# A chunked recurrence followed by a gated MLP: three whole PSUM regions, one step each, and a new order of the pieces

## Chip, cores and metric

One core of a Trainium2 chip runs the kernel; the metric is device microseconds of one execution. Engines are named as in the profile: PE (matmuls), PEld (its weight loads), DVE (VectorE), ACT (ScalarE), POOL (GpSimd), SP (the queue that issues the DMAs).

## The reference

Four batches, eight heads, 768 steps, head size 40. For each batch and head a 40x40 state is carried over the steps; then the outputs of all heads form one row of 320 numbers per step, which goes through a gated MLP.

```
for t in range(768):                       # state: (4, 8, 40, 40)
    y[t]  = r[t] @ state
    Sa    = state @ a[t]
    state = state * w[t] - outer(Sa, b[t]) + outer(v[t], k[t])
h = gelu(x @ w_in); u, v = h[:, :512], h[:, 512:]     # x: 320, h: 1024
out = x + (u * (w_sg @ layernorm(v) * g_ln + b_sg)) @ w_out
```

## The kernel before

The 768 steps are cut into 12 units of 64 (`c` = 0 to 11), and each unit is worked on for four batches (`b` = 0 to 3), eight heads at once. `attention` (L160) builds three kinds of work for a unit.

**Gates**, four per unit, one for each batch (L324 to L407). `gate_w` squares the decays on ACT; `gate_1` scans them on DVE into `ex`; `gate_r` copies the totals to `call` (ACT, into the PSUM tile `fixed[1]`) and takes their reciprocals (DVE); `gate_2` makes `ae`; `gate_3` scans backwards into `hs`, which lies in the same tile `fixed[1]`, makes `kb` (DVE) and issues the load of a later `main`; `gate_4` is 32 matmuls into `pa`, called AB here; `gate_a`, `gate_n` and `gate_k` read AB out of `pa` into `ks` (DVE), `nts` and `kbt` (ACT).

**The inverse**, one per unit for all four batches. `lift` (two ACT copies) and `inv_in` (DVE transposes `nts` into `n`) start a triangular solve of 31 steps. Steps 0 to 28 are a product and an add each on POOL (58 instructions, scratch tile `tg`); the last `LAST` = 2 steps are three small DVE instructions, `by_col` (L446), called column steps here: one scalar_tensor_tensor on 15 or 16 elements for each column that is left. `inv_back` transposes the result twice (`x1z`, `xt`); `inv_g` and `inv_x` are 64 small matmuls each into `pa` (G and X), and `inv_h` and `inv_y` copy them out on ACT (`gs`, `xt`).

**The chain**, fourteen pieces for each unit and batch (`chain`, L645), which carry the state: K and R (`k_mm`, `r_mm`) into `pb`, read by ACT as `past` and `rb`; U into `pb`, read by ACT as `u`; S into `pa`, read by four ACT instructions as `sc`, the state; UT into `pc`, read by ACT as `ut`; P into `pc`, read by DVE as `pqs`; Y into `pc`, read by DVE as `yt`, which SP stores to `xd`. Each of `pa`, `pb`, `pc` is one tile of two PSUM banks, so `pa` serves AB, G, X and S of all batches, `pb` K, R and U, `pc` UT, P and Y.

The order of all this is a list. Each piece has a position (`CHAIN[b]`, `GATE[b]`, `BACK`, `JOIN`, `SOLVE`, `LIFT`, plus 28 per unit); the pieces are sorted by it and tried in turn (L907 to L917). A piece raises `Later` when something it needs has not been issued (`need`) or its place is taken (`take`); it is held and tried again first after every piece that went out. A very early position therefore means "as soon as its needs are met". The instructions of each engine run in the order in which this list emits them. `ahead` (L170) stretches positions below `AHEAD[0]`.

The MLP's preparation (weights split into high and low halves, `Mlp.side`, L1268) is placed in the same list by `DEC`, `PX`, `PV`, `FILL` and others, in the last three units; the MLP itself (`Mlp.run`, L1329) follows in the fixed orders `SEQ0`, `SEQ` and `SEQL`.

```
take("ab", 3)                                   # gate_4: AB's place in pa
take("SP")                                      # s_mm: S's place, also in pa
n = NP * (C + 1)
ones, rc, hsp = fixed[0][:, 0:n], fixed[0][:, n - C:2 * n - C], fixed[1][:, 0:n]
call = fixed[1][:, n:n + NCH * B * NP].rearrange("p (i q) -> p i q", q=NP)
```

Of the kernel before, what the change touches and what calls it, by code (L numbers as in the profile page):

```python
# [32 lines left out]
WARM = 14  # L33
NTS, NX = 4, 3
RING, RING1, FREED = 19, 16, (36, 40)
PZERO = (-30.57, -38.88)
LX = -31.5
LV = -27.58
LR = -24.52
ZERO = (-32.44, -14.72)  # L40
BLANK = (-31.08, -10.75)
IDS = -22.74
HEAT = ((13.9, 11),)
GATE0 = ((0.31, 0, -11.54, -2.54, -8.03, 1.82, 1.17, 2.22, 1.26), (0.03, 0, 0.3, 0.68, -5.12, 1.72, 2.12, 3.36, 2.83))
EW = (1.0, 1.24)
EB = (-31.98, -28.48)
EE = (('GGGG', 'GVGG'), ('GGGG', 'GGGV'))
SUB0 = (-24.73, -24.68, -15.2, -21.18, -15.71)
BACK0 = (-14.34, 0.27)
SOLVE1 = (-14.12, 0.5)  # L50
C10 = -16.81
GATE = ((-91.34, -95.51, -87.94, -87.58, -89.37, -86.29, -82.36, -84.74, -85.37), (-85.42, -83.72, -82.19, -80.33,
    -75.21, -78.25, -71.62, -74.78, -90.65), (-82.7, -77.04, -75.4, -74.24, -72.07, -69.43, -67.72, -63.9, -67.03),
    (-72.51, -74.0, -78.05, -71.52, -74.69, -62.51, -61.13, -75.25, -58.26))
GE = "VVVV"
AHEAD = (19.95, 0.67)
# [10 lines left out]
LIFT = (-59.11, -59.44)  # L67
CG = 0.7978845608028654
G1 = 0.044715
GEND, AEND, IEND = 246.0, (266.0, 294.0), 312.5  # L70
PIN = 266.02
DSTEP = ((-13.06, -3.36, 0.0, 0.13, 3.41, 3.62), (-16.79, -1.11, 0.0, 0.61, 3.02, 3.47))
DEC = ((275.89, 0), (276.24, 0), (284.23, 0), (286.85, 0), (290.7, 1), (297.59, 1), (298.13, 1), (306.35, 0),
    (309.82, 0), (317.07, 1), (323.45, 0), (329.7, 1))
PX = 270.05
PV = 294.03
PL = 335.9
FILL = (("x0", 0, 319.86), ("v0", 0, 331.35), ("v1", 0, 344.98), ("v2", 0, 346.14), ("u0", 0, 349.9))
AFTER = {"v": (0.56, 0.57, 1.47, 1.57, 2.13, 2.48, 2.96, 4.17, 5.19), "u": (1.14, 1.97, 2.82, 3.17), "x": ()}
EARLY = 4  # L80
PSG = 313.1
SGD = (-6.74, -0.32, 1.37)
# [18 lines left out]
JUNK = ((294.28, 5), (295.93, 4), (307.25, 6), (312.36, 3), (312.43, 1), (346.91, 3), (349.9, 4))  # L101
# [58 lines left out]
def attention(tc, a, xd, flag, keep, ps, mlp):  # L160
# [16 lines left out]
    with ExitStack() as ctx:  # L177
# [12 lines left out]
        (pa, pb, pc), slots_end = ps.slots(ctx)  # L190
        fixed, fixed_end = ps.fixed(ctx)

        def gt_end():
            need(*every(("ks", NCH - 1), ("n", NCH - 1), ("kt", NCH - 1)))
            A.copy(out=calls, in_=call.rearrange("p i q -> p (i q)"))
# [13 lines left out]
        mains = static("main", 4, [128, ML], gt)  # L209
# [29 lines left out]
        def main_of(i):  # L239
            return mains[i % 4]  # L240
# [22 lines left out]
        def drop(x):  # L263
            live[x] -= 1

        def warmup(n):
            take("PQ", 0)
            for _ in range(n):
                T.matmul(pc[:, 0, 0:128], lhsT=warm, rhs=warm, start=True, stop=True, skip_group_check=True)
# [30 lines left out]

        spread([lambda: V.memset(pa[:, :, 4 * R104:], 0.0), lambda: V.memset(pb[:, :, 0:4 * D], 0.0), lambda: V.memset(pc, 0.0)] + [lambda t=t: V.memset(t, 0.0) for t in rbs], *PZERO)
        spread([lambda k=k: clear16(xts[k][:, :, 0:32]) for k in range(2)] + [lambda f=f, h=h: clear(f, h) for f in range(2) for h in range(2)], *ZERO)
        spread([lambda: G.memset(gz, 0.0)] + [lambda t=t: G.memset(t, 0.0) for t in scs], *BLANK)

        for i, t in enumerate(aes):
            at(EB[i // 4] + EW[i // 4] * (i % 4 + 0.6) if i < 8 else IDS + i, lambda t=t: A.copy(out=t[:, :, C:C + D], in_=bc(id40.unsqueeze(1), [128, NP, D])))

# [14 lines left out]
        kbs, unit, x1_of, pqt = {}, {}, {}, {}  # L322

        def gate_w(c, b):  # L324
            i = c * B + b
            before(c, b, 4, "kb")
            wv = main_of(i)[:, 1:WL].rearrange("p (q x) -> p q x", x=C + 1)[:, :, 0:C]
            A.activation(out=junk, in_=wv, func=AF.Square, accum_out=wsum[:, i:i + 1])
            seen.add(("w", c, b))

        def gate_1(c, b):
            before(c, b, 4, "kb")
# [5 lines left out]
        def gate_r(c, b):  # L338
            i = c * B + b
            need(("g1", c, b))  # L340
# [13 lines left out]
        def gate_3(c, b, E=V):  # L354
            i = c * B + b
            need(("gr", c, b), ("w", c, b), ("ae", c, b))
            before(c, b, 2, "ab")
            drop("rc")
            w = main_of(i)[:, 0:WL]
# [4 lines left out]
            kb = kbs[c, b] = gt.tile([128, 2, NP, C], F32, name="kb", bufs=2)  # L364
            hv = hs[:, :, 1:C + 1].unsqueeze(1).broadcast_to([128, 2, NP, C])
            E.tensor_tensor(out=kb, in0=kab[:, 0:3:2], in1=hv, op=ALU.mult)
            load_main(i + 4)
# [15 lines left out]
        def pav(x):  # L383
            return pa[:, :, 2 * R104 * x:2 * R104 * x + 2 * R104].rearrange("p h (j w) -> p h j w", j=2)[:, :, :, 0:C]

        def gate_a(c, b):
            need(("ab", c, b))
            before(c, b, RING1, "k")
            V.tensor_tensor(out=kss[ent1(c, b)], in0=pav(0), in1=bc(mask.unsqueeze(1).unsqueeze(1), [128, 2, 2, C]), op=ALU.mult)
            seen.add(("ks", c, b))  # L390
            drop("ab")

        def gate_n(c, b):
            need(("ab", c, b))
            if c >= NTS:
                need(("gp", c - NTS))
            A.mul(out=nts[c % NTS][:, 4 * b:4 * b + 4].rearrange("p (h j) t -> p h j t", h=2), in_=pav(1), mul=-1.0)
            seen.add(("n", c, b))
            drop("ab")

        def gate_k(c, b):
            need(("ab", c, b))
            before(c, b, RING, "yp")
            A.copy(out=kbts[ent(c, b)][:, 0:DM].rearrange("p (h i d) -> p h i d", h=2, i=4),
                   in_=pa[:, :, 0:4 * R104].rearrange("p h (i w) -> p h i w", w=R104)[:, :, :, C:R104])
            seen.add(("kt", c, b))
            drop("ab")  # L407
# [108 lines left out]
        def join16(c):  # L516

            nt, xt = nts[c % NTS], xts[c % 2]
            p = [x.rearrange("p (q t) -> p q t", q=NQ) for x in (pa[:, 0, 0:256], pa[:, 1, 0:256], pa[:, 0, 256:512])]


            def first():
                need(("x1", c))
                take("ab")
# [7 lines left out]
            def lower():  # L532
                need(("j1", c))
                drop("ab")
# [3 lines left out]
            def second():  # L538
                need(("j2", c))
                take("ab", 2)  # L540
# [12 lines left out]
            def add_t():  # L553
                need(("j3", c))
                drop("ab")
# [5 lines left out]
            def add_x():  # L561
                need(("j3", c))
                drop("ab")
# [6 lines left out]
        def inv_back(c, k):  # L570
# [11 lines left out]
            else:  # L582
                need(("x1", c) if c else ("ax", c))
# [17 lines left out]
        def inv_h(c):  # L601
            need(("gp", c), *((("xp", c - 1),) if c else ()))
            drop("ab")
# [5 lines left out]
        def inv_x(c):  # L609
            need(("gs", c), ("xc", c, 0), ("xc", c, 1))  # L610
            take("ab")
# [8 lines left out]
        def inv_y(c):  # L620
            need(("xp", c))
            drop("ab")
# [857 lines left out]
```

## Time and profile before

| | |
|---|---|
| runs (us) | 791.82, 793.41, 802.39; median 793.41 |
| profiled execution (us) | 805.59; its span 803.9 |
| PE busy | 599.9 us (75%), 14292 matmuls |
| DVE busy | 482.4 us (60%), 950 instructions |
| ACT busy | 339.7 us (42%), 1001 instructions |
| POOL busy | 354.3 us (44%), 842 instructions |
| mean granted clock of PE | 0.802 |

Busy time is the time in which an engine has at least one instruction under way. A wait is an engine's idle time in front of an instruction, put down to what released it. The chain that ended last follows the run back from its last instruction, at each step to what released it or to the instruction before it on its engine. The granted clock is the share of PE's full speed; its two levels are 1.2 and 2.4 GHz. The windows view cuts the span into stretches.

### The profile page before, as it was taken

Reading aid. Unit: us, or ns where it says so; the run is one execution under the profiler, and the core shown is the slowest. Engines: PE = TensorE matmul, PEld = TensorE weight load, DVE = VectorE, ACT = ScalarE, POOL = GpSimd, SP = SyncE. Lnnn points to the kernel's source line nnn. Section 1 sums busy time; section 2 is a strip of 40 time slices with the busy share of each in tenths; the row PEclk is TensorE's granted clock in tenths of the full one; section 3 lists DMA queues with packets and bytes.
Section 4 is the critical chain, followed back from the end, with each engine's and each line's share of the span. In section 5 each row is a group of like instructions: output and inputs, shape, how many; then the busy total and the mean of one; then the engine's idle time right before and its main releaser. Section 6 shows DMA issues by size and latency. Waiting matters only on the chain.

```text
span 803.9 us, 32652 instructions
## 1 busy us (share of the span) xinstructions
PE 599.9 (75%) x14292; PEld 555.5 (69%) x14292; DVE 482.4 (60%) x950; ACT 339.7 (42%) x1001; POOL 354.3 (44%) x842
## 2 busy tenths in 40 slices
PE   4445657576758475867576777768799999999997
PEld 4345557575747464767476766656699899999996
DVE  5554774647473837373835244555898876866843
ACT  3543435444444444444443343433644453443520
POOL 4625694636372736372728402022535433323331
PEclk7555667876887888868886666857989999999999
DMA  4411223232323222323112322312420020110001
GB/s 167 126 42 52 73 64 93 65 90 65 90 65 92 63 90 65 93 62 92 47 45 65 93 79 71 106 32 77 145 74 7 25 84 26 36 49 25 25 1 55
DMA packets 38872, 54.58 MB, mean 68 GB/s; under 512 B 19712, under 2 KB 30464, under 8 KB 38720
## 3 DMA queue, kind: packets, MB, share of 16 engines
q1 hardware_dynamic: 38720, 52.40, 22.1%
q8 instruction: 114, 1.87, 1.0%
q14 instruction: 38, 0.31, 0.1%
HBM read 44.52 MB, written 7.86 MB: 65 GB/s over the span
## 4 chain that ended last, share of the span: by engine, by line
PE 57%; DVE 21%; ACT 12%; issue 6%; DMA 1%; POOL 1%; SPq 0%; DVEq 0%; ACTq 0%; POOLq 0%
PE pa L146 15%; PE sg L146 13%; PE pc L146 8%; PE pb L146 7%; PE op L146 5%; PE hv L146 5%; DVE x L146 5%; PE hu L146 4%; DVE pqs L146 2%; DVE ks L146 2%; DVE fixed L146 2%; ACT sc L146 2%; DVE n L146 2%; ACT gs L146 2%; ACT nts L146 1%
## 5 line engine op out<-in xcount | busy, mean ns | idle before, releaser
L146 POOL TENSOR_TENSOR tg<-x,n 128x126 f32<-128x126 f32 (+24 forms) x334 | 118.8, 366 | 177.9 <-DVE n L146 165.2
L146 POOL TENSOR_TENSOR x<-x,tg 128x126 f32<-128x126 f32 (+24 forms) x334 | 120.0, 370 | 12.0
L146 PE MATMUL pa<-ae,kb 64*64 64x104 f32 x1536 | 63.1, 319 | 38.2 <-ACT nts L146 8.0
L146 PEld LDWEIGHTS pa<-ae,kb 64*64 64x64 f32 x1536 | 51.4, 178 | 43.9 <-POOL ae L146 11.7
L146 DVE TENSOR_TENSOR_SCAN fixed<-main,fixed 128x260 f32<-128x260 f32 x42 | 29.1, 693 | 70.7 <-ACT fixed L146 70.4
L146 PE MATMUL sg<-wsh,vh 128*128 128x384 f32 x192 | 66.0, 344 | 4.5 <-ACT wsh L146 4.5
L146 DVE TENSOR_TENSOR pqs<-pc,mask 128x512 f32<-128x512 f32 x48 | 32.9, 685 | 58.9 <-ACT ut L146 34.6
L146 PE MATMUL sg<-wsl,vh 128*128 128x384 f32 x192 | 65.7, 342 | 0.4 <-POOL wsl L146 0.4
L146 PE MATMUL sg<-wsh,vl 128*128 128x384 f32 x192 | 65.6, 342 | 0.0
L146 POOL TENSOR_TENSOR gx<-g,gy 128x384 fp32r<-128x384 f32 x30 | 31.7, 1060 | 64.5 <-ACT gy L146 64.5
L146 PE MATMUL pb<-vs,ks 64*64 64x40 f32 x768 | 43.1, 268 | 13.9 <-ACT u L146 8.8
L146 PEld LDWEIGHTS pb<-vs,ks 64*64 64x64 f32 x768 | 38.9, 181 | 17.0 <-ACT u L146 11.5
L146 ACT ACTIVATE sc<-pa,ex 104x40 f32<-104x40 f32 x176 | 37.2, 296 | 26.0 <-PE pa L146 25.3
L146 PE MATMUL pa<-x1z,nts 32*32 32x32 f32 (+1 forms) x896 | 23.1, 225 | 33.2 <-DVE x1z L146 31.8
L146 ACT COPY rb<-pb 128x320 f32<-128x320 f32 (+1 forms) x48 | 20.1, 418 | 65.1 <-PE pb L146 65.1
L146 POOL TENSOR_TENSOR lt<-lt,sc 128x256 f32<-128x256 f32 (+1 forms) x11 | 6.7, 612 | 90.2 <-ACT lt L146 42.2
L146 PEld LDWEIGHTS pa<-x1z,nts 32*32 32x32 f32 x896 | 21.4, 143 | 34.8 <-DVE x1z L146 33.1
L146 PE MATMUL pc<-rv 64*64 64x64 f32 x768 | 26.0, 257 | 25.4 <-ACT ut L146 24.4
L146 PE MATMUL pc<-rv,rb 64*64 64x64 f32 x704 | 24.8, 270 | 26.2 <-DVE pqs L146 26.2
L146 DVE TENSOR_TENSOR yt<-pc,ex 104x256 f32<-104x256 f32 x48 | 19.5, 407 | 41.1 <-PE pc L146 25.0
L146 PE MATMUL pb<-rb,xt 64*64 64x40 f32 x768 | 40.8, 255 | 3.6 <-ACT rb L146 2.6
L146 DVE SCALAR_TENSOR_TENSOR x<-x,n 128x15 f32<-128x15 f32 (+2 forms) x34 | 42.1, 1242 | 0.4
(169 smaller groups left out, 1772.2 us busy)
## 6 DMA issues: line engine op xcount, KB each, us to landing
main<-main SPq DMA_DIRECT2D x88, 160.8 KB
rv<-rv SPq DMA_DIRECT2D x48, 240.0 KB
vs<-vb SPq DMA_DIRECT2D x24, 160.0 KB
xd<-yt SPq DMA_DIRECT2D x96, 40.0 KB
xt<-xd SPq DMA_DIRECT2D x16, 192.0 KB
out<-y SPq DMA_DIRECT2D x16, 192.0 KB
ws<-wst SPq DMA_DIRECT2D x12, 192.0 KB
main<-first SPq DMA_DIRECT2D x4, 514.5 KB
```

Of the source, the lines that this page charges most:

```text
L146: return self.tc.keep_in_program_order(f(*a, **k))
```

## The change

PSUM: the three two-bank tiles are now three equal regions (`slots` 0, 1, 2), and a table `SLOT` gives every step of every batch one of them whole. `hold` takes the region before the matmuls, `free` gives it up with the last reader. No two steps share a region at a time in the list. `call` moves from `fixed[1]` in PSUM to `calls` in SBUF, so ACT no longer writes the tile that DVE's `hs` scans write; the copy of `call` at the end of the gates is gone.

Buffers: `main` has six tiles in place of four (`NM`; the six are loaded whole at the start), `kb` four in place of two (`NK`), the POOL scratch three in place of two.

Solve: `LAST` = 3, so steps 0 to 27 are on POOL (56 instructions), and six column steps on DVE end it.

Order: all positions of the recurrence are new, most of them far below zero. Clearing the regions and scratch tiles is now something that the first users `need`. `k_mm` waits in the list for S and Y of its own batch in the unit before, in place of U of the batch before; U opens its own accumulation. The 11 warm-up matmuls of `HEAT` are gone. The positions of the MLP's preparation move by a few units at most; the MLP's own order is the same.

```diff
+SLOT = {'AB': [0, 2, 1, 0], 'G': [0], 'X': [1], 'R': [1, 2, 1, 2], 'U': [0, 2, 1, 1], 'SP': [0, 1, 0, 1], 'UT': [2, 1,
+    0, 2], 'PQ': [1, 0, 2, 0], 'YP': [2, 2, 2, 2]}
 NTS, NX = 4, 3
+NM, NK = 6, 4
-HEAT = ((13.9, 11),)
+HEAT = ()
-GATE = ((-91.34, -95.51, -87.94, -87.58, -89.37, -86.29, -82.36, -84.74, -85.37), (-85.42, ...
+GATE = ((-110.27, -128.96, -296.34, -114.57, -150.08, -85.83, -81.69, -262.03, -432.92), (-68.4, ...
-CHAIN = ((-1.17, -5.94, 1.87, -10.45, -4.45, 0.8, 7.4, -4.35, -12.01, 5.4, 15.73, 10.49, 19.51, 3.41), (-6.44, ...
+CHAIN = ((-0.75, -48.5, -87.55, -1.43, -286.58, -131.61, -26.49, -93.14, -58.32, -158.08, 17.2, -33.17, 22.28,
+    -13.06), (-3.03, ...
-SOLVE = (-63.22, -55.95, 0.7)
-LAST = 2
-BACK = (1.65, 3.79, -2.9, 2.67)
-JOIN = (-5.29, -10.98, -6.3, 8.02)
+SOLVE = (-58.31, -50.2, 0.69)
+LAST = 3
+BACK = (-18.88, 3.85, 8.97, -51.07)
+JOIN = (-59.81, -24.91, -46.27, 12.87)
-        mains = static("main", 4, [128, ML], gt)
+        mains = static("main", NM, [128, ML], gt)
-        call = fixed[1][:, n:n + NCH * B * NP].rearrange("p (i q) -> p i q", q=NP)
         calls = keep.tile([128, NCH * B * NP], F32, name="calls")
+        call = calls.rearrange("p (i q) -> p i q", q=NP)
+        def hold(ph, b=0, n=1):
+            need(("pz", SLOT[ph][b]))
+            take(("s", SLOT[ph][b]), n)
+
+        def free(ph, b=0):
+            drop(("s", SLOT[ph][b]))
         def gate_4(c, b):
-            need(("kb", c, b))
-            take("ab", 3)
+            need(("kb", c, b), ("id", ent1(c, b)))
+            ...
+            hold("AB", b, 3)
+            pa = slot("AB", b)
-            R, U, SP = pb[:, :, 0:4 * D], pb[:, :, 4 * D:6 * D], pa[:, :, 4 * R104:4 * R104 + 2 * D]
-            PQ, UT, YP = pc[:, :, 0:4 * C], pc[:, :, 4 * C:6 * C], pc[:, :, 6 * C:8 * C]
+            R, U, SP = slot("R", b)[:, :, 0:4 * D], slot("U", b)[:, :, 0:2 * D], slot("SP", b)[:, :, 0:2 * D]
+            PQ, UT, YP = slot("PQ", b)[:, :, 0:4 * C], slot("UT", b)[:, :, 0:2 * C], slot("YP", b)[:, :, 0:2 * C]
             def k_mm():
                 if c:
-                    need(*([("um", c, b - 1)] if b else every(("um", c - 1))))
-                take("R")
+                    need(("sm", c - 1, b), ("yp", c - 1, b))
+                hold("R", b)
-            fs = chained(c, steps(c, 0, 31 - LAST, G, f"tg{c % 2}"), "in", "so" if LAST else "sv")
+            fs = chained(c, steps(c, 0, 31 - LAST, G, f"tg{c % NX}"), "in", "so" if LAST else "sv")
```

## Rows read from the trace of the kernel before

**Rows 1.** Windows view: busy us of each engine, granted clock, DMA share, in five stretches.

```profile
0.00:66.42 66.42, 31.67 (x764) 28.25 (x764) 36.02 (x90) 29.45 (x82) 34.01 (x112) 0.56 0.32 102
66.42:121.98 55.56, 32.70 (x934) 29.44 (x934) 37.22 (x64) 24.14 (x84) 39.38 (x113) 0.62 0.24 69
...
236.91:276.86 39.95, 26.50 (x1088) 24.45 (x1088) 23.43 (x40) 17.62 (x61) 19.56 (x58) 0.80 0.28 78
...
436.64:534.08 97.44, 71.78 (x2404) 64.94 (x2404) 41.29 (x109) 40.11 (x128) 22.92 (x47) 0.68 0.28 82
...
583.56:803.90 220.34, 213.28 (x1157) 204.42 (x1157) 158.16 (x328) 83.98 (x181) 76.20 (x86) 0.98 0.12 37
```

**Rows 2.** Chain that ended last, in order: start us, us, engine and tile.

```profile
66.42 1.94 PE pa L146 x64
...
121.98 1.94 PE pa L146 x64
...
270.87 3.48 DVE x L146
...
436.64 1.92 PE pa L146 x64
...
534.08 3.65 PE hv L146 x8
```

**Rows 3.** Waits view, 118.8 to 434 us: total us, times, longest.

```profile
DVE fixed L146 <- ACT fixed L146: 57.5, 8, 7.6
...
PE pa L146 <- DVE x1z L146: 25.8, 8, 4.2
...
PE pc L146 <- DVE pqs L146: 16.4, 16, 1.3
```

**Rows 4.** Windows view of tile pa, of pb and of pc, one unit.

```profile
236.91:276.86 39.95, 12.58 (x448) 10.68 (x448) 1.67 (x4) 8.71 (x28) 0.80 0.28 78
...
236.91:276.86 39.95, 9.28 (x256) 8.47 (x256) 0.00 (x0) 3.47 (x12) 0.80 0.28 78
...
236.91:276.86 39.95, 9.24 (x384) 7.94 (x384) 4.29 (x8) 1.56 (x4) 0.80 0.28 78
```

**Rows 5.** Column steps on VectorE: two lines by form, one of the timeline.

```profile
L146 DVE SCALAR_TENSOR_TENSOR x<-x,n 128x15 f32<-128x15 f32 x22 | 32.3, 1473 | 0.0
...
L146 DVE SCALAR_TENSOR_TENSOR x<-x,n 128x16 f32<-128x16 f32 x11 | 9.6, 872 | 0.4
...
506.71 0.52 DVE L146 SCALAR_TENSOR_TENSOR x<-x,n 128x15 f32<-128x15 f32 x2
```

**Rows 6.** Lines by form in one unit, 236.9 to 276.86 us.

```profile
L146 PE MATMUL pa<-ae,kb 64*64 64x104 f32 x128 | 4.9, 287 | 0.6 <-ACT kbt L146 0.4 <-DVE ks L146 0.2
...
L146 DVE TENSOR_TENSOR_SCAN fixed<-main,fixed 128x260 f32<-128x260 f32 x4 | 2.8, 690 | 7.3 <-ACT fixed L146 7.2
...
L146 DVE TENSOR_TENSOR kb<-main,fixed 128x512 f32<-128x512 f32 x4 | 2.7, 686 | 0.1
...
L146 DVE TENSOR_TENSOR pqs<-pc,mask 128x512 f32<-128x512 f32 x4 | 2.7, 685 | 4.4 <-ACT ut L146 3.0 <-PE pc L146 1.4
...
L146 DVE STREAM_TRANSPOSE n<-nts 128x1024 f32<-128x1024 f32 x1 | 2.0, 1972 | 0.0
...
L146 DVE TENSOR_TENSOR ks<-pa,mask 128x256 f32<-128x256 f32 x4 | 1.7, 418 | 2.1 <-ACT nts L146 2.1
...
L146 ACT ACTIVATE nts<-pa 128x256 f32<-128x256 f32 x4 | 1.6, 392 | 0.0
...
L146 ACT COPY nts<-nts 32x512 f32<-32x512 f32 x2 | 1.2, 616 | 0.0
...
L146 DVE STREAM_TRANSPOSE x1z<-x 128x512 f32<-128x512 f32 x1 | 1.0, 1041 | 0.0
```

**Rows 7.** Timeline of POOL: start us, us, instructions merged as xcount, [idle before].

```profile
266.35 0.24 POOL L146 TENSOR_TENSOR tg<-x,n 128x31 f32<-128x31 f32 x1 [18.66 <-DVE n L146]
...
270.60 0.64 POOL L146 TENSOR_TENSOR tg<-x,n 128x91 f32<-128x91 f32 x2
```

More of the change, by code (lines that the diff above doesn't have):

```diff
@@ L189, in attention @@
         gt, gt_right = pool("at_gate", "right")
-        (pa, pb, pc), slots_end = ps.slots(ctx)
+        slots, slots_end = ps.slots(ctx)
         fixed, fixed_end = ps.fixed(ctx)
         def gt_end():
-            need(*every(("ks", NCH - 1), ("n", NCH - 1), ("kt", NCH - 1)))
-            A.copy(out=calls, in_=call.rearrange("p i q -> p (i q)"))
+            need(*every(*[(x, NCH - 1 - k) for x in ("ks", "n", "kt") for k in range(4)]))
             gt_right()
@@ L264, in drop, with slot @@
             live[x] -= 1
+        def slot(ph, b=0):
+            return slots[SLOT[ph][b]]
+        def hold(ph, b=0, n=1):
[3 more added lines that the diff above has]
+            drop(("s", SLOT[ph][b]))
         def warmup(n):
-            take("PQ", 0)
+            take(("s", 2), 0)
             for _ in range(n):
-                T.matmul(pc[:, 0, 0:128], lhsT=warm, rhs=warm, start=True, stop=True, skip_group_check=True)
+                T.matmul(slots[2][:, 0, 0:128], lhsT=warm, rhs=warm, start=True, stop=True, skip_group_check=True)
         warmup(WARM)
@@ L356, in gate_3 @@
             need(("gr", c, b), ("w", c, b), ("ae", c, b))
-            before(c, b, 2, "ab")
+            need(*[("ab", *x) for x in kbo[-NK:len(kbo) - NK + 1]])
             drop("rc")
+            kbo.append((c, b))
             w = main_of(i)[:, 0:WL]
@@ L610, in inv_x @@
             need(("gs", c), ("xc", c, 0), ("xc", c, 1))
-            take("ab")
+            hold("X")
+            gv = square("X")
             xt = xts[c % 2]
@@ L711, in u_mm @@
                 need(("rb", c, b), ("xt", c))
-                take("U")
+                hold("U", b)
                 for j in range(2):
                     for y, h in ORD:
-                        mm(U[rows(y), h, D * j:D * j + D], xt[rows(y), 4 * b + 2 * h + j], right(y, h, j), y, y, not c and not j)
+                        mm(U[rows(y), h, D * j:D * j + D], xt[rows(y), 4 * b + 2 * h + j], right(y, h, j), y, y, not j)
                 seen.add(("um", c, b))
@@ L725, in ut_mm @@
                 need(("rb", c, b), ("xt", c))
-                take("UT")
+                if c:
+                    need(("pm", c - 1, b))
+                hold("UT", b)
                 for j in range(2):
@@ L788, in y_mm @@
                     raise Later
-                take("YP")
+                hold("YP", b)
                 pqs = pqt.pop(b)
@@ L1444, in lay @@
         main[:, :, WL + 256 * j:WL + 256 * (j + 1)] = em(f[k]).reshape(n, 2 * D, 256)
[L1445 removed]
+    first = np.zeros((NM, 2, 64, ML), np.float32)
     first[..., 0:WL] = 1.0
[L1447 removed]
+    first[:, :, 0:D] = main[0:NM].reshape(NM, 2, D, ML)
     def heads(x):
@@ L1456, in lay @@
     w = raw(f["moe_w_in"])
-    out = dict(main=main, first=first.reshape(4, 128, ML), rv=rows, vb=vb,
+    out = dict(main=main, first=first.reshape(NM, 128, ML), rv=rows, vb=vb,
                x0=np.eye(32, dtype=np.float32).reshape(1, 16, 2, 1, 32).transpose(0, 2, 3, 1, 4).repeat(NQ, 2).repeat(4, 0).reshape(128, NQ, 32),
```

181 lines of the change are left out of this document (93 added, 88 removed), and 3 rows, old and new, of the table CHAIN.

## The prediction

> **What bounds the kernel now.** I read the windows view first. From 583.56 us on, PE is busy 213.28 of 220.34 us at a clock of 0.98: the MLP is bound by PE, and the change doesn't touch it. Before that nothing is full. In the unit from 236.91 to 276.86 us PE is busy 26.5 of 39.95 us, DVE 23.4, POOL 19.6, ACT 17.6 [rows 1]. Then the chain that ended last: X of unit 0 starts at 66.42 us, X of unit 1 at 121.98, X of unit 9 at 436.64, and the first MLP matmul (hv) that follows the last unit at 534.08 [rows 2]. So eight units take 314.7 us, 39.3 each; the start takes 66.4, unit 0 takes 55.6, and the tail 97.4.
>
> What a unit of 39.3 us waits for stands in the waits view. Over eight units PE stood 25.8 us ahead of G for DVE's `x1z` (3.2 a unit) and 16.4 for `pqs`; DVE stood 57.5 us, 7.2 a unit, in front of `hs` scans for an ACT instruction that writes `fixed`, the tile of the scan [rows 3]. That ACT instruction is the copy to `call`. AB's matmuls wait for `kbt` and `ks`, the readers of the AB before, because all use `pa` [rows 6]. POOL stood 18.66 us in one piece for `n`, which comes at the end of the gates [rows 7]. So the unit is set by engines that pass work on in an unlucky order, through three tiles of which one carries most.
>
> How much one carries: PE, DVE and ACT work on `pa` for 12.6 + 1.7 + 8.7 = 23.0 us a unit, on `pb` for 12.8, on `pc` for 15.1 [rows 4].
>
> **The regions.** The table deals the 30 steps of a unit out as 9, 10 and 11. Priced by the old tiles (23.0/10 for a step of `pa`, 12.8/8 for `pb`, 15.1/12 for `pc`), region 0 gets 5 x 2.3 + 1.6 + 3 x 1.26 = 16.9, region 1 18.1, region 2 15.9 us [rows 4]. The fullest region falls from 23.0 to 18.1. Neither is a bound at 39 us; what the deal buys is that the next step on PE mostly goes to another region while ACT reads the last. By the positions, the run after X is U0 (region 0), UT1 (1), U1 (2), S0 (0), U2 (1), UT0 (2), UT2 (0), S1 (1), S2 (0), the digit behind a step being its batch: two steps on other regions lie between nearly all neighbours in one.
>
> **The scans' bank.** With `call` in SBUF the 7.2 us a unit of [rows 3] have no cause left: the new `hs` scan needs only DVE's own results. This is no gain by itself, since DVE is not full; it brings `kb` and so AB, `nts` and `n` earlier.
>
> **The column steps.** One more solve step goes from POOL to DVE: two POOL instructions less, three DVE instructions more. POOL is not full, so the first is worth nothing. A column step took 32.3 + 9.6 us for 33, mean 1.27; the same instruction after POOL had ended took 0.26 (0.52 for two) and the longest piece of the chain is 3.48 [rows 2, 5]. While POOL works, then, a column step is slow. I take 1.27 for each of six, 7.6 us a unit, because POOL will work beside them as it does now; the bounds are 0.26 and 3.48. The Trainium skill ("SBUF — State Buffer", section "Who interferes with whom") says that a DVE instruction with two SBUF inputs and a GpSimd instruction that reads SBUF exclude each other, and that the later one waits until the first is done. By that rule a column step would wait for one POOL instruction at most; the trace disagrees, since no POOL instruction of [rows 7] is near 3.48 us. The sum goes by the row; the rule's own result is a rival below.
>
> **One turn of a unit.** The new order puts the six column steps of unit 5 right behind the last POOL instruction of its solve. On DVE, in order, there follow `x1z` of unit 5, scan and `kb` of gate 7.3 (unit 7, batch 3), reciprocal, scan and `kb` of gate 7.1, two `pqs`, a gate scan and the three `ks` of unit 7. AB 7.1, 7.2, 7.3 run on PE meanwhile, then `nts` and `lift` on ACT, then `n` of unit 7 on DVE, and only then POOL can begin solve 7. So what waits behind a late column step is the whole gate of two units on. The sum:
> (1) column steps 7.6, `x1z` 1.0, two scans 1.4, two `kb` 1.4, a reciprocal 0.2 (estimate): 11.6 us.
> (2) three AB at 4.9/4 = 1.2: 3.7.
> (3) `nts` 0.4, two `lift` copies 1.2, `n` 2.0, and some six hand-overs, 0.3 together (estimate): 3.9. `n` is done at 19.2 us [rows 5, 6].
> (4) The rest of DVE's unit: 23.4 less today's column steps, 4.9 (3.8 us of them on 15 elements at twice the length of the mean, 1.1 on 16; I estimate 3 x 1.6), is 18.5; of that 9.1 stood in (1) to (3) (`x1z` 1.0, scans 1.4, `kb` 1.4, `n` 2.0, two `pqs` 1.4, three `ks` 1.25, a gate scan 0.7) [rows 1, 6]. 9.4 are left: 28.6 us.
> (5) In (4) DVE waits for PE three times (two Y and the last P behind G and R). A step of `pc` is 9.24/12 = 0.8 us of PE [rows 4]; two ahead and a hand-over are 1.7, three times 5.1.
> A unit then takes 33.7 us; I use 33.5. PE's 26.5 fit in it with 7 us of waits where it has 13.4 now. From below: POOL's turn, (1) to (3) and then 16 pairs of instructions, each 0.64 us [rows 7], 10.2 together, before the next column steps: 29.4. From above: DVE's waits other than the 7.2 stay, 39.95 - 23.4 - 7.2 = 9.3, on 18.5 + 7.6: 35.4.
> Eight units at 39.3 - 33.5 = 5.8: 46 us gained (31 to 79).
>
> **The start.** The list now holds 13 AB ahead of X 0, where it had 9, and 4 instead of 8 between X 0 and X 1. DVE has room for them: it is busy 36.0 of the first 66.4 us. A gate costs DVE some 2.8 us (scan, `hs` scan, `kb`, `ks`, and the two small ones), so unit 0 loses 4 x 2.8 = 11 of its 55.6 us, and more by the order. I take 39 for it, a slow unit, since the clock is 0.62 there [rows 1]: 16 us gained, between 8 (the 11 less a later X 0) and 22 (unit 0 as long as the others). Two more `main` loads stand ahead of `vb`, `rv` and `x0` on SP's queue; DMA is busy 0.32 of this stretch [rows 1] and none of the three is needed before the first AB has been read, so I give them nothing. The new loads that gates issue later are the same ones, two units' worth earlier. Clearing three whole regions on DVE comes ahead of the first scan, beside the first load; without that cover two more passes over 1024 elements cost 4 x 0.69 = 2.8 us, by the 512 elements of `kb` [rows 6]. The warm-up matmuls removed and the copy of `call` removed are off the path.
>
> **The tail.** From X 9 to hv no gate is left; PE is busy 71.8 of 97.4 us at 0.68 [rows 1], so 25 is the most that the order can give. The chain through `pc` (UT, P, Y of one batch, then the next) is broken up as in any unit, but the MLP's preparation, unchanged, fills DVE and ACT. I take half of the room less a little, 14 (0 to 25). The MLP starts as much earlier as the tail ends.
>
> **Sum.** The profiled execution took 805.59 us; less 16 + 46 + 14 = 76 it is 729.6. The median of the runs is 793.41, 0.985 of it, so I predict 718.6, say 719. With units from 31.5 to 35.4 and the other terms at their middle bounds the likeliest case alone is 690 to 745.
>
> **Rivals.** *The waits stay and only change their names* (chance 0.13): PE's 13.4 us of idle time less 3.2 ahead of G stay, and a unit takes 36.7; 8 x 2.6 + 16 + 4 gives 41 and so 753. For it: each hand-over costs the same as before. Against: 7.2 us of DVE's wait lose their cause.
> *Column steps are cheap* (0.10): each waits for one POOL instruction at most, 0.26 + 0.32, so six take 3.5 in place of 7.6, and a unit 29.4; 8 x 9.9 + 30 gives 109 and 686. The Trainium skill's rule above speaks for this case. For it: POOL is in its single stage then, with gaps between dependent instructions. Against: the mean of 33.
> *The change doesn't do what it says* (0.08): the three tiles were not what held the steps, PE's order was, and a unit stays within 1 us of 39.3; then only the start is gained, 8 to 16 us, which is within 2%.
> *Column steps starve* (0.09, slower): POOL works without gaps and each of six takes 3.48 us as the worst piece did [rows 2]. They stand in the loop through `n`, so all of it lands on the unit: 33.5 + 6 x 2.21 = 46.8, 8 x 7.5 = 60 us lost, 30 gained at start and tail, 823. It decides from 2.85 us a step on, where a unit is 43 us and the loss eats the 30. For it: six in a row, ahead of the gate. Against: in the trace one of three is that long.
>
> **Numbers.** Likeliest 0.60, then 0.13, 0.10, 0.08, 0.09. Faster by over 2%, about what a measurement of this kernel can tell from no change, means under 777: 0.60 + 0.13 + 0.10 = 0.83; within 2% 0.08; slower 0.09. The range is 680 to 770: it holds the first three cases and leaves out about 0.2.
>
> **What would show it.** After: X to X of the middle units 31.5 to 35.5 us; no wait of `hs` for ACT; PE's wait ahead of G under 1 us; six column steps of 7 to 8 us a unit, and POOL ending a solve just ahead of them; X 1 near 105 us; granted clock in the units at or above 0.80. I am wrong if DVE stands in front of the column steps for POOL, if column steps pass 2.85 us, or if PE's waits for ACT's readers grow to 13 us again.

## The result and the profile after

The changed kernel took 725.81 us (median of 4 runs, 721.31 to 727.75), the kernel before 796.62 on the same chip: 0.910 of it, 95% interval 0.902 to 0.918. The profiled execution took 727.75 us, its span 725.9, at a mean granted clock of 0.848 (before: 805.59, 803.9 and 0.802).

Windows view of the changed kernel (start and end, us, busy us of PE, PEld, DVE, ACT, POOL, granted clock, DMA share, GB/s), cut at X of unit 0, 1, 9 and at the first MLP matmul:

```profile
0.00:68.50 68.50, 34.86 (x892) 31.59 (x892) 50.49 (x114) 36.82 (x104) 44.77 (x138) 0.63 0.39 134
68.50:102.45 33.95, 24.58 (x886) 23.04 (x884) 23.79 (x46) 19.21 (x68) 27.22 (x78) 0.71 0.30 79
102.45:366.04 263.59, 200.76 (x8660) 185.53 (x8660) 170.18 (x315) 141.64 (x475) 159.00 (x448) 0.86 0.32 86
366.04:454.85 88.81, 65.07 (x2308) 58.86 (x2308) 45.23 (x114) 40.17 (x124) 24.45 (x49) 0.71 0.31 86
454.85:725.90 271.05, 251.29 (x1535) 236.25 (x1535) 190.41 (x397) 106.59 (x229) 95.56 (x108) 0.96 0.16 47
```

Against [rows 1, 2]: X of unit 0 is 2.1 us later, unit 0 takes 33.95 us instead of 55.56, eight units take 263.6 instead of 314.7 (32.95 each, before 39.3), the tail 88.8 instead of 97.4; what follows hv is 1.2 us longer. That is 19.5 + 51.1 + 8.6 - 1.2 = 78.0 us of span.

Waits of the same eight units (engine, line, tile, what released it: us in total, times, longest):

```profile
POOL tg L151 <- ACT x L151: 89.1, 8, 13.6
DVE yt L151 <- PE pc L151: 38.1, 23, 4.2
PE pb L151 <- issue: 17.5, 15, 2.0
PE pc L151 <- issue: 16.5, 15, 2.9
DVE pqs L151 <- PE pa L151: 14.3, 10, 3.4
PE pa L151 <- issue: 12.1, 13, 2.3
PE pb L151 <- ACT past L151: 4.6, 16, 0.5
```

DVE's 57.5 us for ACT in the scans' bank and PE's 25.8 us for `x1z` ahead of G, both in [rows 3], are not in the list any more. DVE now waits for PE. PE's largest waits, 46.1 us together, are "issue": the profile names no releaser. Where it names a reader of a region, as `past`, PE waits 0.6 us at most, but for one wait of 1.5 us for `nts`.

The column steps, and DVE's other instruction that reads two SBUF tiles, `ae`, in the lines by form of the whole run (busy us, mean ns):

```profile
L151 DVE TENSOR_TENSOR ae<-main,ex 128x256 f32<-128x256 f32 x40 | 25.2, 647 | 0.7
L151 DVE SCALAR_TENSOR_TENSOR x<-x,n 128x15 f32<-128x15 f32 x55 | 14.0, 319 | 1.0 <-POOL x L151 1.0
L151 DVE SCALAR_TENSOR_TENSOR x<-x,n 128x16 f32<-128x16 f32 x11 | 4.8, 439 | 0.4
```

One turn of DVE in the timeline (start us, us; xcount instructions merged; [idle before]):

```profile
239.78 1.88 DVE L151 SCALAR_TENSOR_TENSOR x<-x,n 128x15 f32<-128x15 f32 x6
241.70 1.08 DVE L151 STREAM_TRANSPOSE x1z<-x 128x512 f32<-128x512 f32 x1
...
244.90 0.69 DVE L151 TENSOR_TENSOR kb<-main,fixed 128x512 f32<-128x512 f32 x1
247.05 0.69 DVE L151 TENSOR_TENSOR pqs<-pb,mask 128x512 f32<-128x512 f32 x1 [1.47 <-PE pb L151]
...
254.08 2.05 DVE L151 STREAM_TRANSPOSE n<-nts 128x1024 f32<-128x1024 f32 x1 [0.52 <-ACT nts L151]
...
271.84 1.85 DVE L151 SCALAR_TENSOR_TENSOR x<-x,n 128x15 f32<-128x15 f32 x6
```

A column step takes 0.32 us on 15 elements where it took 1.47 [rows 5]; the six of a unit take 1.9 us, not 7.6.

### The profile page after: what moved, and what is told of

Same layout as the page of the kernel before. It is cut to its first block, busy times and chain, and to the rows that moved or that the text cites. A ratio compares the mean times of both kernels' runs of the same rounds, so it can differ in the third digit from the quotient of the medians.

```text
span 725.9 us, 32627 instructions
## 1 busy us (share of the span) xinstructions
PE 576.6 (79%) x14270; PEld 535.3 (74%) x14270; DVE 480.1 (66%) x983; ACT 344.4 (47%) x1000; POOL 351.0 (48%) x820
## 4 chain that ended last, share of the span: by engine, by line
PE 64%; DVE 13%; issue 13%; ACT 7%; POOL 1%; DMA 1%; SPq 0%; ACTq 0%; DVEq 0%; POOLq 0%
PE pc L151 12%; PE pb L151 12%; PE sg L151 12%; PE pa L151 10%; PE op L151 6%; PE hv L151 6%; PE hu L151 5%; ACT sc L151 2%; DVE fixed L151 1%; DVE ex L151 1%; ACT nts L151 1%; PE idle L151 1%; DVE sc L151 1%; DMA rv<-rv 1%; DVE kb L151 1%
## 5 line engine op out<-in xcount | busy, mean ns | idle before, releaser
L151 POOL TENSOR_TENSOR tg<-x,n 128x120 f32<-128x120 f32 (+14 forms) x323 | 116.4, 369 | 110.2 <-ACT x L151 91.7
L151 POOL TENSOR_TENSOR x<-x,tg 128x120 f32<-128x120 f32 (+14 forms) x323 | 118.6, 377 | 13.9
L151 PE MATMUL pc<-pqs,kbt 64*64 64x64 f32 x1536 | 39.8, 245 | 9.7 <-issue 9.2
L151 PEld LDWEIGHTS pc<-pqs,kbt 64*64 64x64 f32 x1536 | 34.3, 159 | 11.2 <-issue 10.4
L151 PE MATMUL pa<-ae,kb 64*64 64x104 f32 x768 | 28.7, 296 | 15.2 <-POOL kb L151 4.6
L151 PEld LDWEIGHTS sg<-wsh,vh 128*128 128x128 f32 x192 | 36.6, 191 | 5.2 <-ACT wsh L151 4.8
L151 PEld LDWEIGHTS sg<-wsl,vh 128*128 128x128 f32 x192 | 36.6, 191 | 1.0 <-POOL wsl L151 0.8
L151 PEld LDWEIGHTS sg<-wsh,vl 128*128 128x128 f32 x192 | 36.6, 191 | 0.0
L151 ACT ACTIVATE q<-q 128x384 f32<-128x384 f32 (+1 forms) x56 | 31.7, 567 | 8.3 <-DVE q L151 8.1
L151 DVE TENSOR_TENSOR_SCAN ex<-main,fixed 128x260 f32<-128x260 f32 x48 | 32.3, 681 | 0.6 <-issue 0.3
```

The lines of the kernel that those rows point to most:

```text
L151: return self.tc.keep_in_program_order(f(*a, **k))
```

## The experiments

"Unit" is the mean distance of DVE's transposes `xt` from unit 1 to unit 8 (seven distances); PE busy and idle are the windows view of that stretch, divided by seven. Ratios are to the kernel before, with 95% intervals.

| kernel | ratio | unit | PE busy | PE idle | clock |
|---|---|---|---|---|---|
| before | 1 | 39.6 | 26.6 | 13.1 | 0.80 |
| changed | 0.910 (0.902-0.918) | 33.3 | 25.0 | 8.3 | 0.86 |
| a_old_order | 1.139 (1.125-1.153) | 54.0 | 37.6 | 16.3 | 0.52 |
| a_old_places | 1.013 (1.006-1.020) | 40.9 | 30.0 | 10.8 | 0.70 |
| b_steps_early | 0.975 (0.967-0.983) | 36.4 | 26.8 | 9.6 | 0.80 |
| b_call_sbuf | 0.988 (0.979-0.997) | 39.3 | 27.5 | 11.8 | 0.77 |
| b_no_pairs | 0.970 (0.959-0.981) | 36.7 | 26.5 | 10.2 | 0.82 |
| a_steps_late | 0.971 (0.962-0.981) | 38.0 | 26.9 | 11.1 | 0.76 |
| a_call_psum | 0.919 (0.912-0.927) | 32.8 | 25.3 | 7.5 | 0.86 |
| a_last2 | 0.909 (0.902-0.915) | 32.8 | 24.8 | 8.0 | 0.87 |
| a_rv | 0.910 (0.904-0.917) | 33.1 | 25.7 | 7.5 | 0.84 |
| a_no_pairs | 0.901 (0.893-0.909) | 33.0 | 25.1 | 8.0 | 0.86 |
| a_best | 0.903 (0.896-0.910) | 32.6 | 25.7 | 6.9 | 0.84 |
| a_bufs_tail | 0.992 (0.987-0.996) | 38.4 | 27.0 | 11.4 | 0.76 |

The theory (A) was that regions and order are worth little without each other; the rivals, that the regions (B) or the order (C) carry the gain alone.

**The new regions with the old order: a_old_order.** All positions are those of the kernel before, MLP positions too; regions, `call` in SBUF, buffers and what the pieces `need` of each other are the new ones.

```
-CHAIN = ((-0.75, -48.5, -87.55, ...
+CHAIN = ((-1.17, -5.94, 1.87, ...        # and all other positions of before
-LAST = 3
+LAST = 2
 SLOT = {'AB': [0, 2, 1, 0], ...           # unchanged
```

> The changed kernel with the three regions, the call row in SBUF and the six main buffers, but every position of the steps (and the MLP's) as in the kernel before. Theory A, the regions and the order are worth little without each other: most of the gain needs both, the unit (from one X to the next) lies between 35.5 and 38 us, the time between 750 and 775 us; VectorE's wait of 57.5 us for ScalarE's copy in the scans' bank is gone all the same. Rival B, the regions alone carry the gain and the order only follows: units of 32.5 to 34 us, 720 to 740 us. Rival C, the order alone carries it: units of 38.5 to 39.5 us and 775 to 797 us. The six (here three) VectorE column steps go back to POOL's pair phase here and cost 0.9 to 1.5 us each against 0.31 in the changed kernel.

It took 922.96 us, slower by 14%: worse than every theory. The windows view of the seven units in a_old_order:

```profile
107.91:485.81 377.90, 263.54 (x7576) 235.21 (x7573) 140.16 (x267) 127.67 (x427) 142.82 (x415) 0.52 0.19 55
```

And their waits:

```profile
POOL tg L149 <- DVE n L149: 222.3, 7, 32.6
...
PE pc L149 <- DVE yt L149: 20.2, 28, 1.7
PE pb L149 <- ACT u L149: 13.1, 7, 1.9
PE pc L149 <- DVE ks L149: 9.0, 7, 1.3
PE pc L149 <- ACT past L149: 7.2, 7, 1.1
```

PE again and again stands for up to 1.9 us in front of the reader that empties a region. With places a tile held several steps side by side (R and U, or P, UT and Y); with whole regions one step holds two banks until its last reader, and the old positions put the next holder of that region right behind. The clock is 0.52, so the same matmuls take 37.6 us a unit instead of 25.0: of the 20.7 us more than in the changed kernel, 12.6 are matmuls at a lower clock and 8.1 idle time. Three whole regions, dealt out in this way, are a cost until the order is made for them; a deal made for the old order was not tried, nor the old order without the new condition of `k_mm`.

One expectation failed here: that the column steps, back beside POOL's two solves, cost 0.9 to 1.5 us each. They took 0.30 (a line by form, then the timelines of DVE and of POOL):

```profile
L149 DVE SCALAR_TENSOR_TENSOR x<-x,n 128x15 f32<-128x15 f32 x22 | 5.7, 301 | 0.0
...
208.28 0.87 DVE L149 SCALAR_TENSOR_TENSOR x<-x,n 128x15 f32<-128x15 f32 x3
...
208.16 0.60 POOL L149 TENSOR_TENSOR tg<-x,n 128x96 f32<-128x96 f32 x2
208.73 0.64 POOL L149 TENSOR_TENSOR x<-x,tg 128x96 f32<-128x96 f32 x2
```

POOL works on two solves in turn there, without a gap (the first two instructions end at 208.76, the next begin at 208.73), and three column steps run beside it at 0.29 us each.

**The new order in the old places: a_old_places.** G, X and S of all batches and AB go to the first tile, R and U to the second, PQ, UT and YP to the third, in the column ranges of before.

```
-        return slots[SLOT[ph][b]]
+        t, lo, hi = PLACE[ph]
+        return slots[t][:, :, lo:hi]
...                                        # hold and free take the place likewise
+PLACE = {'AB': (0, 0, 512), 'G': (0, 0, 512), 'X': (0, 0, 512), 'SP': (0, 416, 512), 'R': (1, 0, 160),
+    'U': (1, 160, 240), 'PQ': (2, 0, 256), 'UT': (2, 256, 384), 'YP': (2, 384, 512)}
```

> The changed kernel in all, its order too, but each step writes where the kernel before had it: gate products, G, X and SP in the first region, R and U in the second, PQ, UT and YP in the third. Theory A, order and regions need each other: the three PE waits for a region come back, units of 35 to 39 us, 750 to 790 us. Rival C, the order alone carries the gain: units under 34 us, 720 to 740 us. Rival B, the regions alone: the order made for the other deal is worse than the old one in these places, units over 39.5 us, more than 797 us.

814.7 us, 1.3% slower than before. PE's waits in its seven units:

```profile
PE pc L153 <- DVE pqs L153: 15.5, 13, 2.0
PE pa L153 <- ACT sc L153: 14.6, 16, 1.0
PE pa L153 <- DVE ks L153: 9.0, 7, 1.3
PE pb L153 <- ACT xt L153: 9.0, 14, 1.1
```

The waits for a place are back under new names. Both kernels have the new buffers and `call` in SBUF. So neither these regions nor this order as a whole give anything alone, +14% and +1.3%; together -9%. Rival C falls here, rival B by a_old_order, though what B forecast for this run came (units over 39.5 us, more than 797 us): the order made for the other deal is worse than the old one in these places. Theory A had the direction, and both times lie above its ranges (750 to 775 and 750 to 790 us).

**Earlier column steps in the kernel before: b_steps_early.** One position; the order is otherwise that of before.

```
-BACK = (1.65, 3.79, -2.9, 2.67)
+BACK = (-18.88, 3.79, -2.9, 2.67)
```

> The kernel before, with one position changed: VectorE's three column steps of a unit and the transpose behind them are put where the changed kernel has them, ahead of the unit's products, so that they run in POOL's single stage. Theory on the price: a column step's length is set by what POOL does beside it (0.31 us beside the single stage as in the changed kernel, up to 3.48 us beside the pair phase), so the two sizes, 128x15 and 128x16, fall from means of 1473 and 872 ns to under 500 ns. What it is worth: if the column steps were on the path, about 3 us a unit, so 760 to 780 us; rival, their place was free because the products of the turn and the waits for regions set the unit: 785 to 800 us; third, the earlier steps hold VectorE when the products' sums wait for it and the time rises to 800 to 815 us.

782.19 us, 2.5% faster. From 120 to 355 us the column steps take 310 ns on 15 elements and 344 on 16; in the kernel before 1650 and 950 in the same stretch. That is 2 x 1.34 + 0.61 = 3.3 us a unit, and the unit is 3.2 us shorter. The first theory holds for the unit; the time lies 2 us above its range, between it and the rival's. `ae` rose from 468 to 872 ns, since DVE now reaches it while POOL alternates; the unit got shorter all the same.

**One solve at a time on POOL: b_no_pairs.** In the kernel before POOL's instructions of two solves alternate for part of a unit: the end of one and the start of the next, which is the row of two instructions in [rows 7]. The edit forbids that; the orders of DVE and ACT are those of before, instruction by instruction.

```
         need((first if not k else last + str(k), c))
+        if not k and last[:2] == "so" and c > 1:
+            need(("so", c - 1))
```

> The kernel before with one condition added: POOL begins the solve of a unit only behind the last step of the solve of the unit before, so POOL never has the steps of two solves in turn. The order on DVE in the units, the column steps' place among it, the regions and the gates stay. Theory of the gaps: DVE's column step reads both inputs from SBUF and gets in only between two POOL instructions; two solves in turn leave no gap (rows of two instructions, 0.58 to 0.66 us, that follow each other without one), one solve leaves some 0.08 us behind each instruction. Then the column steps, in the old place, fall from 1473 and 872 ns to under 400 ns, 3 us a unit less, 765 to 785 us, as the earlier steps gave (782). Rival, it is the place and not POOL's stage that makes them slow (they wait for something POOL has not yet done): they keep their length, and the time stays at 785 to 805 us or rises.

777.58 us, 3.0% faster. Lines by form of DVE in b_no_pairs:

```profile
L146 DVE SCALAR_TENSOR_TENSOR x<-x,n 128x15 f32<-128x15 f32 x22 | 5.7, 268 | 0.0
L146 DVE SCALAR_TENSOR_TENSOR x<-x,n 128x16 f32<-128x16 f32 x11 | 3.8, 349 | 0.4
```

Its timeline, POOL beside two column steps of DVE:

```profile
260.45 0.38 POOL L146 TENSOR_TENSOR x<-x,tg 128x100 f32<-128x100 f32 x1
260.91 0.35 POOL L146 TENSOR_TENSOR tg<-x,n 128x96 f32<-128x96 f32 x1
261.34 0.38 POOL L146 TENSOR_TENSOR x<-x,tg 128x96 f32<-128x96 f32 x1
...
261.06 0.71 DVE L146 SCALAR_TENSOR_TENSOR x<-x,n 128x15 f32<-128x15 f32 x2
```

And POOL's timeline in the kernel before, right behind the row of [rows 7]:

```profile
271.19 0.65 POOL L146 TENSOR_TENSOR x<-x,tg 128x91 f32<-128x91 f32 x2
271.81 0.61 POOL L146 TENSOR_TENSOR tg<-x,n 128x78 f32<-128x78 f32 x2
```

The same column steps, in the same place of DVE's order, fall from 1473 to 268 ns and from 872 to 349, with POOL working beside them. From 260.83 to 260.91 and from 261.26 to 261.34 POOL is free: a dependent instruction follows after 0.08 us. In the kernel before, the two instructions of [rows 7] end at 271.24 and the next two begin at 271.19, the two after these at 271.81: no gap. Without the alternation, two independent streams on POOL, no column step is long: the long ones need it, and their place in DVE's order is not enough. The rival falls. One condition gave a third of what the whole change gave.

The alternation is not enough either. In a_old_order the steps are cheap beside it, and so is the first of the three in the unit of [rows 7], beside instructions of POOL that follow each other without a gap (DVE's timeline):

```profile
266.99 0.23 DVE L146 SCALAR_TENSOR_TENSOR x<-x,n 128x15 f32<-128x15 f32 x1
```

The long steps don't end at a gap that the trace shows: the one of 3.48 us [rows 2] and one of 2.34 us, from 153.23 us in the same chain, both end 8.0 us behind the first POOL instruction of their alternation (266.35 and 147.56), with POOL still busy. In the kernel before and in a_old_order every step that began within 4 us of that instruction took 0.22 to 0.52 us. What in the alternation decides is left open.

**Late column steps in the changed kernel: a_steps_late.**

```
-BACK = (-18.88, 3.85, 8.97, -51.07)
+BACK = (5.4, 3.85, 8.97, -51.07)
```

> The changed kernel with one position changed: VectorE's six column steps of a unit and the two transposes behind them are put 24.28 positions later, where VectorE does them while POOL is in its pair phase. Theory on the price (a column step is 0.3 us beside POOL's single stage and 1 to 1.5 us beside its pair phase): their mean rises from 0.33 us to over 1 us, six of them from 1.9 us to 6 to 9 us a unit. That stretch is on the path, since the transposed sums are what the next products of the unit start from: units of 36.5 to 40 us against 33, 755 to 790 us. Rival, the chain of products sets the unit and the column steps have room: units of 33 to 34 us, 722 to 735 us.

772.39 us: the time is in the range of the first theory, its reason is not. The column steps stayed cheap, 413 ns on 15 elements and 280 on 16: in most units DVE reached them when POOL had left the alternation (where one `ae` took 3.24 us instead), and two of the units in which it had not have a step of 2.24 and one of 3.26 us. What cost 5 us a unit is that `x1z` and `xt` come late; waits of the seven units in a_steps_late:

```profile
ACT xt L151 <- DVE xt L151: 34.4, 7, 6.6
PE pa L151 <- DVE x1z L151: 27.6, 7, 5.6
```

The wait for `x1z` of [rows 3], which the changed kernel doesn't have, is back at 3.9 us a unit. So the early place of the six column steps and their transposes is worth about 6% of the time for its place alone.

**The scans' bank: b_call_sbuf and a_call_psum.** The same edit in both directions; the last copy of `call` at the end of the gates goes or comes with it.

```
-call = fixed[1][:, n:n + NCH * B * NP].rearrange("p (i q) -> p i q", q=NP)    # ScalarE's copy in the scans' bank
+call = calls.rearrange("p (i q) -> p i q", q=NP)                              # in SBUF
```

> The kernel before, with one edit: ScalarE's small copy of the gate sums goes to SBUF instead of into the bank of the scans, order and places unchanged. The wait of VectorE for ScalarE ahead of the scan (57.5 us in the middle of the kernel before) falls under 10 us in every theory. If it was on the path that sets a unit: 2 to 5 us a unit less, 755 to 780 us. Rival, VectorE then waits for the next thing (the products' regions), and the unit stays: 787 to 800 us.

793.4 us, 1.2% faster, units shorter by 0.4 us. DVE's waits of the seven units in b_call_sbuf:

```profile
DVE yt L146 <- issue: 56.1, 7, 9.9
```

The wait for ACT is gone and 56.1 us, for which the profile names no releaser, stand ahead of `yt` in its place: the rival holds for the units.

> The changed kernel with ScalarE's small copy of the gate sums back in the bank of the scans, nothing else. In the kernel before the same edit the other way gave 1.2%. Theory A: VectorE's wait for ScalarE ahead of the scan comes back at 20 us or more over the eight middle units and part of it is on the path: 730 to 745 us. Rival: the order of the changed kernel leaves the two apart, the wait stays under 10 us and the time within 720 to 730 us.

731.2 us, 0.919 against 0.910, and the intervals overlap. The time lies in theory A's range. DVE waits 20.6 us for ACT in front of the scans, over the whole run (theory A: 20 or more in the eight units alone), but the units are no longer than the changed kernel's (32.8 us), so this wait is not on the path of a unit. What the profiled execution takes more lies at the start: `xt` of unit 1 comes at 98.03 us instead of 92.14, and from there to the end it takes 632.0 us, the changed kernel 633.8.

**The split of the solve: a_last2.**

```
-LAST = 3
+LAST = 2
```

> The changed kernel with three column steps of a unit on VectorE instead of six (the split of before); POOL does the other three as pairs. Theory on the price: VectorE is freed of 0.9 us a unit and POOL takes 2.2 us more (three pairs of about 0.73 us), a stretch that ends in the transpose. If that stretch is on the path: 1 to 1.5 us a unit more, 735 to 745 us. Rival, POOL's stage has room (it waits 89 us for ScalarE in the eight middle units): 722 to 730 us.

722.89 us: no difference from the changed kernel that these runs can tell. The rival holds: POOL has room.

**The same condition in the changed kernel: a_no_pairs.** The edit is that of b_no_pairs.

> The same condition in the changed kernel. There the column steps already run beside one solve (0.33 us each); what still runs beside two is the gate product of DVE with both inputs in SBUF (ae, mean 0.78 us in the units where it takes 0.42 alone, 4 a unit). Theory of the gaps: ae falls to 0.4 to 0.5 us, 1 to 1.5 us a unit of DVE; since PE's order is on the path, the time falls by less, 712 to 725 us. Rival, the first step of a solve is now later behind the last one of the solve before and the next unit's X waits for it: 730 to 750 us.

723.39 us, the same. `ae` fell from 647 to 507 ns over the run; the units stay at 33.0 us. Behind its own order the alternation costs the changed kernel nothing, since what it slows has room.

**The tail: a_rv, a_best.** In the changed kernel the last but one unit takes 41.8 us from `xt` to `xt`. PE's wait there, in the waits of 366.04 to 454.85 us:

```profile
PE pb L151 <- DMA rv<-rv: 9.4, 2, 9.0
```

POOL and SP's queue in the timeline:

```profile
409.51 0.73 POOL L151 TENSOR_TENSOR lt<-lt,sc 128x256 f32<-128x256 f32 x1 [27.09 <-ACT lt L151]
411.19 0.80 POOL L151 TENSOR_TENSOR wil<-stg,lt 128x256 fp32r<-128x256 f32 x1
...
391.15 12.38 SPq L151 DMA_DIRECT2D stg<-w  x2
412.02 0.33 SPq L151 DMA_DIRECT2D stg<-w_in  x1
412.40 0.73 SPq L151 DMA_DIRECT2D rv<-rv  x2
```

SP's load of MLP weights waits for a stage buffer that POOL gives back at 411.99, and the loads of `rv` stand behind it on SP's queue. a_rv issues two stage loads behind them:

```
-            at(DEC[k][0] + d, lambda k=k, i=i: step(k, i))
+            at(DEC[k][0] + d + (9.4 if k in (5, 6) and not i else 0.0), lambda k=k, i=i: step(k, i))
```

> The changed kernel with one edit: of the twelve loads into the three stage buffers for the MLP weights, two (the sixth and the seventh in the list) are issued 9.4 positions later, behind the two rv loads of the second last unit on SP's queue, not ahead of them. Theory on the tail: the load that waits for a stage buffer holds the rv loads behind it on the queue, which is why TensorE waits 9.0 us for rv at 412.80 to 417.67; the wait falls under 2 us and 5 to 9 us of the end go with it: 716 to 721 us. Rival: the wait only moves (a stage, a vb load or the weights of the MLP are late next) and the time stays at 723 to 728 us.

724.15 us, the same as the changed kernel. Waits of the tail in a_rv:

```profile
ACT sc L151 <- DMA stg<-w_in: 4.7, 1, 4.7
...
PE pc L151 <- ACT past L151: 8.4, 2, 5.7
```

The wait for `rv` is gone, and the rival is right: ACT now stands 4.7 us for the stage load, with `past` behind it in its order, and PE waits for `past`. a_best also moves the two conversions, and takes the split of a_last2:

```
-LAST = 3
+LAST = 2
-DEC = (..., (290.7, 1), (297.62, 1), (298.27, 1), ...
+DEC = (..., (290.7, 1), (301.62, 1), (304.27, 1), ...      # and their loads by 5.4 and 3.1 more
```

> The changed kernel with three column steps on DVE instead of six and with the sixth and the seventh weight conversion of the MLP moved by 4 and 6 positions, their loads by 9.4 and 9.1, so that both stage loads stand behind the rv loads on SP's queue and ScalarE reaches the conversion later. Theory on the tail: the wait that moved from TensorE (for rv, 9.0 us) to ScalarE (for the stage, 5 us) when the loads alone were moved goes too; the last but one unit falls from 41.9 to 36 to 38 us, 715 to 720 us. Rival, the MLP's weights come late in its place and the time stays at 721 to 726 us.

723.35 us. The last but one unit still takes 42.2 us, and ACT waits for two stage loads:

```profile
ACT sc L152 <- DMA stg<-w: 4.9, 1, 4.9
ACT sc L152 <- DMA stg<-w_in: 4.7, 1, 4.7
```

The rival holds again. No kernel of the study is faster than the changed one by more than these runs can tell.

**Fewer buffers, and the tail once more: a_bufs_tail.**

```
-NM, NK = 6, 4
+NM, NK = 4, 2
-DEC = (..., (290.7, 1), (297.62, 1), ...
+DEC = (..., (290.7, 0), (297.62, 1), ...                   # and the loads of a_rv
```

> The changed kernel with two edits in stretches that don't overlap. For the start and the units, main buffers and kb buffers back to four and two (six and four in the changed kernel). For the tail, the two stage loads behind the rv loads and the fifth weight conversion on VectorE instead of POOL, so that the stage buffer for which SP waited on POOL's wil in the last but one unit is freed by VectorE. Theory on the buffers: the loads are early anyway, the transpose xt of unit 1 ends within 1.5 us of where it does with six and four (90 to 92 us), and the units stay at 32.5 to 33.5 us; rival, the gates ahead of X of unit 0 wait for a main buffer and that time is 5 us or more later. Theory on the tail: TensorE's wait for rv (9.0 us) and ScalarE's for the stage load (4.7 us) are both gone, the last but one unit falls from 39.7 to 41.9 us to 36 to 38, and the time with unchanged start is 716 to 720 us; rival, what sets that unit is the number of MLP instructions on ScalarE and VectorE, a wait only changes its name again, and the unit stays at 40 us or more.

790.49 us: nearly all of the gain is gone. `xt` of unit 1 comes at 120.46 us instead of 92.14, and a unit takes 38.4 us. Waits of a_bufs_tail, 95 to 370 us:

```profile
PE pa L151 <- DVE ks L151: 30.6, 7, 5.1
DVE ex L151 <- DMA main<-main: 25.6, 7, 4.2
```

Once a unit DVE stands 3.7 us in front of a gate scan for its `main`, with `ks` behind it, and PE stands for `ks`. The changed kernel has no wait for `main`. My theory on the buffers fell, and its rival was too mild: it is 28 us at the start and 5 us a unit. Fewer buffers also make the list issue pieces in another order, so the load's wait and the other order can't be told apart here. On the tail: from `xt` of unit 8 to the end it takes 392.6 us, the changed kernel 400.9; the last but one unit takes 38.9, the wait for `rv` is gone. With the gates in another order too, I don't call that shown.

## Why the prediction was right, and where its steps were not

719 us were predicted with a range of 680 to 770, and "faster" with 0.83; 725.81 were measured. The eight units were predicted at 33.5 us and took 32.95. But this sum hit for partly wrong reasons, and that it hit so closely is luck: 16 + 46 + 14 = 76 us were forecast, 19.5 + 51.1 + 8.6 - 1.2 = 78.0 measured, and inside the unit two errors cancel.

**The column steps were mis-sized.** The term of 7.6 us a unit (1.27 each) measured 1.9 (0.31). The reason "POOL will work beside them as it does now" was the wrong step: I took POOL as working or not, and a mean that mixes 0.23 and 3.48 us as the price of its work. In the old place POOL alternated between two solves; in the new one, about 6 us behind the alternation, it doesn't, and b_no_pairs shows that without the alternation the steps are cheap in the old place too. The price was that of the rival *column steps are cheap*. The sign "POOL ending a solve just ahead of them" came 6 us off: the turn was not as tight as it was drawn. The Trainium skill ("SBUF — State Buffer", section "Who interferes with whom") has a DVE instruction with two SBUF inputs and a GpSimd instruction that reads SBUF exclude each other, the later one waiting for the earlier. The single stage agrees with it: 0.31 us beside POOL instructions of about 0.4. In the alternation the kernel before does not, if one takes "waits for one instruction" from it: 3.48 us in [rows 2] beside two instructions in 0.64 [rows 7]; a_old_order does, with 0.29 us. What decides between the two, the runs don't show.

**The waits of a turn were too small.** With the right price the sum would have been 33.7 - 5.7 = 28.0 us; 32.06 were measured for the turn from 239.78 to 271.84. Part (1) without the column steps' error was good: 5.9 us by the sum, 5.8 measured to the end of the second `kb`. Parts (2) and (3), 7.6 us, measured 10.5 (245.59 to the end of `n` at 256.13): DVE waits there for PE and ACT, 1.47 us ahead of one `pqs` alone. Parts (4) and (5), 14.5 us, measured 15.7. The two errors, 5.7 too much and 4.1 too little, cancel but for 1.6. DVE's work doesn't set the unit: DVE freed of 0.9 us (a_last2) or of slow `ae` (a_no_pairs) gave nothing. That PE's order sets it is argued, not shown; most of PE's waits have no releaser in the profile.

**The regions.** "Neither is a bound at 39 us" was too short a check. I summed the busy time of a region's steps, 16.9 to 18.1 us a unit; a step holds its region until its last reader, and with the old order the unit took 54 us. "What the deal buys is that the next step on PE mostly goes to another region" was right, and it is the new order that makes it so. The rival *the change doesn't do what it says* named PE's order as what held the steps: the order alone, in the old places, didn't free them either.

**The scans' bank.** Right: the wait is gone and is "no gain by itself". b_call_sbuf gave 0.4 us a unit, and the wait reappeared ahead of `yt`.

**The buffers** got no term beyond the two earlier loads at the start. That step failed silently: the 13 AB ahead of X of unit 0 and the turn of the units both lean on six `main` buffers. With four, and the list that follows from them, 28 us at the start and 5 us a unit are lost.

**The start** was put at 16 us and gave 19.5: X of unit 0 is 2.1 us late (0 assumed), unit 0 took 33.95, not 39. **The tail** was put at 14 and gave 8.6: SP's queue, where a stage load held up `rv` for PE's 9.0 us, was not in the sum, but a_rv, without this wait, gained nothing: what holds the tail is open.

**What was to show it:** X to X within 31.5 to 35.5 (32.95), no wait of `hs` for ACT, no wait of PE ahead of G, X of unit 1 near 105 (102.45), a clock of at least 0.80 (0.86) all came; six column steps of 7 to 8 us and a solve that ends just ahead of them did not.

## What to carry to other kernels

Price an instruction by what stands beside it at its new place, one by one and not by the mean of a form: the mean of 1.27 us stood for steps of 0.23 and of 3.48. Beside one dependent chain on the other engine they were all cheap here; beside two in turn some were not. Scratch dealt out in whole regions, the order of the work and the number of load buffers are one choice: here the first two, without the other, cost 14% and 1.3%, and with it and the buffers gave 9%. A wait that is taken away shows what was queued behind it: follow it (the bank's wait to `yt`, `rv` to the stage load) before you book it as gain.

## What the chip showed that was not expected

A VectorE instruction that reads two SBUF tiles took up to 3.88 us (the longest column step of the kernel before) beside POOL instructions of 0.3 us that follow each other without a gap, and 0.27 in the mean beside POOL instructions of 0.4 us with gaps of 0.08 between them (b_no_pairs). But in a_old_order it took 0.30 in the mean beside the stream without gaps: the missing gap alone doesn't make it slow.

TensorE's clock multiplies what an order costs. The same matmuls of a unit took 25.0 us at a granted clock of 0.86, 26.6 at 0.80, 30.0 at 0.70 and 37.6 at 0.52, which is near the lower of its two levels. PE's idle time in a unit (8.3, 13.1, 10.8 and 16.3 us) doesn't order them by itself; in the last it came in many waits of up to 1.9 us.

PE's largest waits in the changed kernel, 46.1 us in eight units, have no releaser in the profile. What they are is left open.
